# A routed expert layer on one core: the order of gathers, block products and weight loads around the second product

## The chip, the cores and the metric

The kernel runs on one core of a Trainium2 chip. The metric is the device time of one execution in microseconds (us); shown are the median of three executions and, from one further execution, a profile taken by the hardware profiler. TensorE (PE in the profile; its weight loads are PEld), VectorE (DVE), ScalarE (ACT) and GpSimd (POOL) each work through their own instructions in order and wait for one another by semaphores; SyncE (SP) only issues transfers.

## The reference

Linear attention without softmax gives 4608 rows of 512 numbers, and each row then goes through one of eight two-layer networks ("experts"), which a gate chooses:

```python
kv = einsum('bhsd,bhse->bhde', k, v)
out = einsum('bhsd,bhde->bhse', q, kv)
x = out / sqrt(mean(out * out, -1) + 1e-6) * g_norm      # rearranged to (4608, 512)
e_idx = argmax(x @ w_gate, 1)
gate_w = softmax probability of that expert
eom = sigmoid(x @ w_output_gate)
for e in range(8):
    mask = e_idx == e
    h = maximum(x[mask] @ w1[e], 0)        # 512 -> 1024
    out[mask] = gate_w * eom[mask, e] * (h @ w2[e])   # 1024 -> 512
```

All is fp32.

## The kernel before, in words

The first third (`p1_main`) computes the attention and the gate, and writes each row, with its norm factors and its scale, to a table in HBM. What the change touches comes after it, in the loop over `RUNS` at line 1225. A run is the work of one expert on its rows, in the order of how many rows the experts have: runs 0 and 1 share the first expert, runs 2 to 8 take the other seven, with 672, 632, 608, 592, 576, 576 and 544 rows. A run has three kinds of work.

**Rows.** `gather` (line 239) fetches the rows of a run by indirect DMA that GpSimd issues, one per tile of 128 rows, into the buffers `xg`. `scale_rows` (262, by `scale_heads`, 257) multiplies them on GpSimd by their norm factors, one instruction a tile. `settle` (250) is a drain on GpSimd behind the last gather; in this loop it is called for the rows of run 8, in run 7. `x_stage` (410) transposes two tiles on TensorE and splits them and the block sums into a rounded high part (ScalarE) and the remainder (VectorE); `x_sums` (472) splits the sums. Both run in the second product of the run before.

**First product.** fp32 is made from two rounded parts: high x high, high x low, low x high. The first product, `x @ w1`, is done by a scheme of seven block products in place of eight (`seven`, 488) over four chunks c of the hidden columns. It is a generator; each step issues one block product of six matmuls (`product`, 480) with what ScalarE and VectorE make of it. For a chunk the order is 11, S3, 12, S2, then `late3` and `late4` of the chunk before, then S1; chunk 0 has five steps, the others seven, and two steps, `late3(3)` and `late4(3)`, close the generator. `late3` adds to the accumulator `a`, of which ScalarE must have copied S1's value (`sn`, 550); `late4` adds to `d`, which VectorE must have read (551). The sums of W1's blocks are made on GpSimd (`w_sums`, 366, four instructions a chunk), and `w_split` (377) splits W1 and the sums.

**Second product.** `mm2` (562) goes over the row tiles of a run; for each of eight hidden blocks f it issues three matmuls into one of two PSUM buffers `y0`, `y1`, and behind them whatever was put down as the events of f. Then y is scaled to SBUF and scattered to the output by an indirect DMA on GpSimd. A last tile of at most 64 rows (`half`; runs 1, 2, 6, 7 and 8) has two halves in PSUM that are added, with a buffer `y2`.

The order is written out by hand. `begin(i, n)` issues n steps of run i's products; `put(tile, f, ...)` puts work into the events. In run i the first loop (1251) issues chunks 1 to 3 of the first product, with the split of W2's chunk (`split`, 203), the load of the next W1 (`wload`, 195, issued by SP), in chunk 2 the gathers of run i + 1, and in chunk 3 the sums of the next W1's chunk 0 and the scaling. `listing` (1143) is a generator of small VectorE steps for a list of overflowing experts. Chunk 0 of the next run's product is issued in the events of the last tile.

The buffers of W1, W2, their splits, `xg`, `sn`, `ct`, `y2` and others are 29 slots of one size. `take` (173) hands out the one that has been free longest in the order of the code, and the new user's instruction waits until the old user's last reader is through. So the order of the code also settles what a load or a gather waits for.

Of the kernel before, what the change touches and what calls it, by code (L numbers as in the profile page):

```python
# [135 lines left out]
def body(ctx: ExitStack, tc: tile.TileContext, kvm, rem, qT, wg, gn, w1, w2, kc, xs, tab, out):  # L136
# [425 lines left out]
    def mm2(i, k, events):  # L562
# [37 lines left out]
        if M == T:  # L600
            y2_ = take([P, 1024], F32, "y2")
            y2 = y2_[:, 0:DM]
            o = T if i > 1 else P // 2
            nc.scalar.copy(y2[:M], ps[o:o + M])
            nc.vector.tensor_tensor(out=y[:M], in0=ps[:M], in1=y2[:M], op=ALU.add)
            nc.vector.tensor_scalar(out=y[:M], in0=y[:M], scalar1=tl[:M, 0:1], scalar2=None, op0=ALU.mult)
            give(y2_)
        else:
            nc.scalar.activation(y[:M], ps[:M], AF.Copy, scale=tl[:M, 0:1])  # L609
# [4 lines left out]
        tc.add_to_no_dep_group("out", i_.ins)  # L614
        return i_
# [596 lines left out]
    with tc.manual_schedule(engines=MAN):  # L1212
# [12 lines left out]
        for i in range(len(RUNS)):  # L1225
# [23 lines left out]
            else:  # L1249

                for c in range(4):
                    if c:
                        begin(i, 2)
                        split(p, 2, c)
                        begin(i, 4)
                        if change:
                            wload(p + 1, 1, c - 1)
                        begin(i, 1)
                    else:
                        split(p, 2, c)  # L1260
                    if c == 2 and not last_run:
                        g_ = gather(i + 1)
                        if i + 2 == len(RUNS):
                            settle(g_)
                    if c == 3 and not last_run:
                        sums_of(p + 1, 0)
                        scale_rows(i + 1)
                    next(listing, None)
                    next(listing, None)
# [7 lines left out]
            if last_run and half(i):  # L1277
                order.insert(1, order.pop())
            if i > 1:
                put(order[0], 1, begin, i, 1)  # L1280
                put(order[0], 3, begin, i, 1)
                if change:
                    put(order[0], 3, wload, p + 1, 1, 3)
            if change:
                for c in range(4):
                    if c:
                        put(order[c - 1], 0, sums_of, p + 1, c)
# [4 lines left out]
                put(order[T - 1], 0, wload, p + 1, 2, 0)  # L1292
                for f, n in ((1, 1), (3, 2), (5, 1), (7, 1)):
                    put(order[T - 1], f, begin, i + 1, n)
# [9 lines left out]
            if i > 0:  # L1304
                for c in range(4):
                    drop(2, c)
            if change:
                for c in range(1, 4):
                    wload(p + 1, 2, c)
# [105 lines left out]
```

## Time and profile before

| | us |
|---|---|
| median of three executions | 585.17 (584.56 to 586.82) |
| the profiled execution | 586.47 |
| its span, first to last instruction | 584.7 |
| mean granted clock of TensorE | 0.975 of full speed |
| TensorE busy | 545.3 |
| VectorE busy | 378.5 |
| ScalarE busy | 299.4 |
| GpSimd busy | 258.4 |

Run 2's products begin in the last tile of run 1, near 178 us; the second product of run 7, with 8's first steps in it, ends near 535 us. How to read it: a row of the timeline has its start from the span's start, its duration, the engine, the line of the kernel and the operation; what stands in brackets is how long the engine stood idle before it and which instruction's end released it. A row of waits sums these idle times by waiting and releasing line. The granted clock is the share of its full speed of 2.4 GHz that TensorE was given in a stretch; 0.50 is its lower level of 1.2 GHz. A duration of matmuls is modelled at its end, so starts are the better guide.

### The profile page before, as it was taken

The numbers are of one execution on the slowest core, as the hardware profiler recorded it, in microseconds if no ns is written. First come the engines' busy times: TensorE is split into PE (matmuls) and PEld (weight loads), VectorE is DVE, ScalarE is ACT, GpSimd is POOL, SyncE is SP. The second block draws the span as 40 slices with busy tenths as digits, with TensorE's granted clock in tenths as the row PEclk, the third lists the DMA queues.
The fourth block names the chain that finished last, engine by engine and source line by source line (L and its number), as shares of the span: only waits on it lengthen the run. The fifth ranks groups of instructions, "written<-read, shape, count | busy, mean of one in ns | idle before, by whom it ended". The sixth has DMA issues, their size and how long they took to land.

```text
span 584.7 us, 10991 instructions
## 1 busy us (share of the span) xinstructions
PE 545.3 (93%) x4052; PEld 464.2 (79%) x4052; DVE 378.5 (65%) x897; ACT 299.4 (51%) x632; POOL 258.4 (44%) x280
## 2 busy tenths in 40 slices
PE   8899989999899969989999999989998999699995
PEld 6688877748788948879789878978896788588974
DVE  2135998855697798267955793669278947494610
ACT  1468764332575537245645482657365645374510
POOL 2001323178472466237743772487148722781011
PEclk9999997998999989999999999999999999799999
DMA  8999999945004600254054305511551236023001
GB/s 263 372 417 415 416 395 336 343 154 189 1 38 158 219 24 36 91 184 159 19 189 135 121 36 180 189 53 57 195 167 38 90 132 220 0 89 129 2 20 46
DMA packets 28744, 92.35 MB, mean 158 GB/s; under 512 B 4082, under 2 KB 4210, under 8 KB 28688
## 3 DMA queue, kind: packets, MB, share of 16 engines
q1 hardware_dynamic: 21952, 71.63, 33.6%
q0 software_dynamic: 6304, 19.78, 9.7%
q8 instruction: 33, 0.54, 0.4%
q10 hardware_dynamic: 432, 0.21, 0.1%
q14 instruction: 23, 0.19, 0.1%
HBM read 72.41 MB, written 19.78 MB: 158 GB/s over the span
## 4 chain that ended last, share of the span: by engine, by line
PE 56%; DVE 17%; DMA 11%; ACT 7%; issue 4%; POOL 2%; POOLq 1%; SPq 0%; DVEq 0%; ACTq 0%
PE yps L596 26%; PE hpsa L484 11%; PE hpsd L484 4%; DVE hT L507 4%; DMA ld<-kvm 3%; PE hps L484 3%; PE yps L590 3%; ACT hT L504 2%; PE yps L574 2%; PE tps L430 2%; DMA xs<-xrow 2%; DMA ld<-rem 2%; DVE wlo L229 2%; DMA wraw<-w 2%; PE ops L792 2%
## 5 line engine op out<-in xcount | busy, mean ns | idle before, releaser
L596 PE MATMUL yps<-whi,hT 128*128 128x512 f32 (+3 forms) x560 | 188.7, 401 | 7.9 <-ACT hT L504 4.8
L596 PEld LDWEIGHTS yps<-whi,hT 128*128 128x128 f32 (+3 forms) x560 | 104.7, 188 | 35.6 <-ACT hT L504 7.4
L610 POOL DMA_INDIRECT out<-y,oidx x42 | 57.3, 1365 | 164.7 <-ACT y L609 119.5
L596 PE MATMUL yps<-wlo,hT 128*128 128x512 f32 (+3 forms) x280 | 110.9, 396 | 0.0
L244 POOL DMA_INDIRECT xg<-xs,gidx x42 | 46.3, 1103 | 55.6 <-DMA xs<-xrow 14.4
L507 DVE SCALAR_TENSOR_TENSOR hT<-ct,hT 128x256 fp32r<-128x256 f32 (+6 forms) x88 | 46.3, 557 | 22.8 <-ACT hT L504 22.8
L596 PEld LDWEIGHTS yps<-wlo,hT 128*128 128x128 f32 (+3 forms) x280 | 52.6, 188 | 9.9
L504 ACT ACTIVATE hT<-ct 128x288 fp32r<-128x288 f32 (+11 forms) x56 | 34.6, 618 | 43.0 <-DVE ct L518 43.0
L229 DVE TENSOR_TENSOR wlo<-wraw,whi 128x1024 fp32r<-128x1024 f32 x32 | 43.5, 1359 | 12.3 <-ACT whi L226 12.2
L609 ACT ACTIVATE y<-yps,tl 128x512 f32<-128x512 f32 (+3 forms) x37 | 25.3, 685 | 49.3 <-PE yps L596 19.8
L484 PE MATMUL hpsa<-xT,wh 128*128 128x288 f32 (+5 forms) x224 | 48.1, 302 | 1.5 <-ACT sn L542 1.1
L484 PE MATMUL hpsd<-xT,wh 128*128 128x288 f32 (+5 forms) x224 | 48.0, 301 | 0.3 <-DVE xT L477 0.3
L484 PE MATMUL hpsa<-xb,wh 128*128 128x288 f32 (+5 forms) x224 | 47.6, 300 | 0.6 <-DVE hT L507 0.6
L818 DVE TENSOR_REDUCE ss<-sq 128x8 f32<-128x512 f32 x36 | 23.9, 681 | 33.2 <-ACT sq L808 33.2
L260 POOL TENSOR_TENSOR xg<-xg 128x512 f32<-128x512 f32 (+6 forms) x40 | 43.6, 1122 | 0.0
L792 PE MATMUL ops<-aug,ld 64*128 64x80 f32 (+1 forms) x640 | 41.5, 283 | 0.0
L388 DVE SCALAR_TENSOR_TENSOR wl<-wraw,gcol,wh 128x512 fp32r<-128x512 f32 (+1 forms) x56 | 40.7, 766 | 0.0
L484 PEld LDWEIGHTS hpsa<-xT,wh 128*128 128x128 f32 x224 | 37.1, 188 | 4.0 <-ACT sn L542 1.3
L484 PEld LDWEIGHTS hpsa<-xb,wh 128*128 128x128 f32 x224 | 37.2, 188 | 2.2 <-DVE hT L507 0.9
L792 PEld LDWEIGHTS ops<-aug,ld 64*128 64x128 f32 (+1 forms) x640 | 36.3, 188 | 3.1 <-issue 1.2
L484 PEld LDWEIGHTS hpsd<-xT,wh 128*128 128x128 f32 x224 | 37.2, 188 | 2.0 <-DVE xT L477 0.6
L388 DVE SCALAR_TENSOR_TENSOR wl<-ws,gcol,wh 128x1024 fp32r<-128x1024 f32 x28 | 38.1, 1360 | 0.1
(222 smaller groups left out, 1142.1 us busy)
## 6 DMA issues: line engine op xcount, KB each, us to landing
wraw<-w SPq DMA_DIRECT2D x64, 512.0 KB, 3.8
ld<-kvm SPq DMA_DIRECT2D x32, 512.0 KB, 9.9
ld<-qT SPq DMA_DIRECT2D x18, 512.0 KB, 10.5
xs<-xrow SPq DMA_DIRECT2D x9, 528.0 KB, 6.6
xs<-xrow SPq DMA_DIRECT2D x2, 1320.0 KB, 6.5
xs<-xrow SPq DMA_DIRECT2D x1, 2112.0 KB, 12.7
ld<-rem SPq DMA_DIRECT2D x3, 512.0 KB, 9.9
xg<-xs,gidx POOLq DMA_INDIRECT x42, 4.2
```

Source lines behind the costliest of these rows:

```text
L229: eng.tensor_tensor(out=lo, in0=r, in1=hi.bitcast(F32), op=ALU.subtract)
L244: gathered = nc.gpsimd.indirect_dma_start(out=x[:M, :], out_offset=None, in_=rows, in_offset=bass.IndirectOffsetOnAxis(ap=gidx[:M, p, t:t ...
L260: eng.tensor_tensor(out=v, in0=v, in1=f, op=ALU.mult)
L388: nc.vector.scalar_tensor_tensor(out=lo, in0=x, scalar=gcol[:, 0:1], in1=hi.bitcast(F32), op0=ALU.mult, op1=ALU.subtract)
L484: nc.tensor.matmul(ps, W[a][d], X[b][d], start=start and k == 0, stop=k == 5, skip_group_check=not start)
L504: S.activation(hh, x, AF.Relu)
L507: V.scalar_tensor_tensor(out=v(o, j1 - j0), in0=x[..., j0:j1], scalar=0.0, in1=hh[..., j0:j1].bitcast(F32), op0=ALU.max, op1=ALU.subtract)
L596: nc.tensor.matmul(ps[:M], a, b, start=(f == 0 and j == 0), stop=(f == 7 and j == 2))
L609: nc.scalar.activation(y[:M], ps[:M], AF.Copy, scale=tl[:M, 0:1])
L610: i_ = nc.gpsimd.indirect_dma_start(out=out, out_offset=bass.IndirectOffsetOnAxis(ap=oidx[:M, p, t:t + 1], axis=0), in_=y[:M], in_offset=N ...
L792: nc.tensor.matmul(v[r0:r0 + m, u, p, :], qt[g // 2][r, p, q0:q0 + m], augs[b % 3][r, p, :], start=True, stop=True)
L818: nc.vector.tensor_reduce(out=o, in_=sq, axis=AX.X, op=ALU.add)
```

## The change

The gathers of run i + 1 are issued after the split of chunk 2 and ahead of four more block products; the scaling follows in the same chunk and no longer behind the sums of W1's chunk 0. `late3(3)` and `late4(3)` come at events 0 and 1 of the first tile instead of 1 and 3, and the sums of W1's later chunks at event 1 instead of 0. The loads of W1's chunks come a chunk later, the last two together at event 1. In the last tile, W2's chunks are dropped at events 1, 3 and 5, each followed by the load of a chunk of the next W2; before, three of the loads came after the tile. The last step of chunk 0 of the next run (S1) comes in new events "8", behind y and its scatter. The half tile's y is scaled in the two instructions that add it, and the third is gone. The list's steps are one for each of chunks 1 to 3, where they were two for each of chunks 0 to 3.

```diff
@@ -601,9 +601,9 @@
             y2_ = take([P, 1024], F32, "y2")
             y2 = y2_[:, 0:DM]
             o = T if i > 1 else P // 2
-            nc.scalar.copy(y2[:M], ps[o:o + M])
-            nc.vector.tensor_tensor(out=y[:M], in0=ps[:M], in1=y2[:M], op=ALU.add)
-            nc.vector.tensor_scalar(out=y[:M], in0=y[:M], scalar1=tl[:M, 0:1], scalar2=None, op0=ALU.mult)
+            nc.scalar.activation(y2[:M], ps[o:o + M], AF.Copy, scale=tl[:M, 0:1])
+            nc.vector.scalar_tensor_tensor(out=y[:M], in0=ps[:M], scalar=tl[:M, 0:1], in1=y2[:M],
+                                           op0=ALU.mult, op1=ALU.add)
             give(y2_)
         else:
             nc.scalar.activation(y[:M], ps[:M], AF.Copy, scale=tl[:M, 0:1])
@@ -612,6 +612,8 @@
             in_=y[:M], in_offset=None, bounds_check=NTOK - 1, oob_is_err=False)
         tc.declare_no_dep(i_.ins, group="out", reason=nodep)
         tc.add_to_no_dep_group("out", i_.ins)
+        for e in events.get(8, ()):
+            e()
         return i_
 
 
@@ -1252,21 +1254,22 @@
                     if c:
                         begin(i, 2)
                         split(p, 2, c)
+                        if c == 2 and not last_run:
+                            g_ = gather(i + 1)
+                            if i + 2 == len(RUNS):
+                                settle(g_)
                         begin(i, 4)
-                        if change:
-                            wload(p + 1, 1, c - 1)
+                        if change and c > 1:
+                            wload(p + 1, 1, c - 2)
                         begin(i, 1)
                     else:
                         split(p, 2, c)
                     if c == 2 and not last_run:
-                        g_ = gather(i + 1)
-                        if i + 2 == len(RUNS):
-                            settle(g_)
-                    if c == 3 and not last_run:
+                        scale_rows(i + 1)
+                    if c == 3 and change:
                         sums_of(p + 1, 0)
-                        scale_rows(i + 1)
-                    next(listing, None)
-                    next(listing, None)
+                    if c:
+                        next(listing, None)
 
             at = {}
 
@@ -1276,22 +1279,27 @@
             order = list(range(T))
             if last_run and half(i):
                 order.insert(1, order.pop())
+            end = order[T - 1]
             if i > 1:
+                put(order[0], 0, begin, i, 1)
                 put(order[0], 1, begin, i, 1)
-                put(order[0], 3, begin, i, 1)
                 if change:
-                    put(order[0], 3, wload, p + 1, 1, 3)
+                    for c in (2, 3):
+                        put(order[0], 1, wload, p + 1, 1, c)
             if change:
                 for c in range(4):
                     if c:
-                        put(order[c - 1], 0, sums_of, p + 1, c)
+                        put(order[c - 1], 1, sums_of, p + 1, c)
                     put(order[c], 4 if c < T - 1 else 0, w_split, p + 1, c)
                 for k in range(3):
                     put(order[k], 2, x_stage, i + 1, k)
                     put(order[k], 7, x_sums, i + 1, k)
-                put(order[T - 1], 0, wload, p + 1, 2, 0)
-                for f, n in ((1, 1), (3, 2), (5, 1), (7, 1)):
-                    put(order[T - 1], f, begin, i + 1, n)
+                put(end, 0, wload, p + 1, 2, 0)
+                for c in range(3):
+                    put(end, 2 * c + 1, drop, 2, c)
+                    put(end, 2 * c + 1, wload, p + 1, 2, c + 1)
+                for f, n in ((1, 1), (3, 2), (5, 1), (8, 1)):
+                    put(end, f, begin, i + 1, n)
             for k in order:
                 g_ = mm2(i, k, at.get(k, {}))
                 if last_run and k == order[-3]:
@@ -1303,10 +1311,8 @@
                     stage(1, k)
             if i > 0:
                 for c in range(4):
-                    drop(2, c)
-            if change:
-                for c in range(1, 4):
-                    wload(p + 1, 2, c)
+                    if (2, c) in wgt:
+                        drop(2, c)
     main.close()
 
     with ExitStack() as p3:
```

## Rows read from the trace of the kernel before

**Rows 1.** The page: busy us (share of the span) and instructions of each engine.
```profile
PE 545.3 (93%) x4052; PEld 464.2 (79%) x4052; DVE 378.5 (65%) x897; ACT 299.4 (51%) x632; POOL 258.4 (44%) x280
```

**Rows 2.** Waits of PE, 180 to 560 us: us in total, times, longest us.
```profile
PE tps L430 <- POOL xg L260: 8.8, 8, 6.0
PE yps L596 <- ACT hT L504: 4.8, 4, 3.8
PE yps L596 <- DVE hT L507: 2.8, 4, 1.3
PE hps L484 <- DVE y L605: 2.5, 4, 0.7
PE hpsa L484 <- ACT sn L542: 1.1, 1, 1.1
PE hpsa L484 <- DVE hT L507: 0.6, 1, 0.6
PE hpsa L484 <- ACT sn L532: 0.3, 2, 0.2
```

**Rows 3.** Stretches: PE, PEld, DVE, ACT, POOL busy us, granted clock, DMA share, GB/s.
```profile
217.50:221.50 4.00, 3.89 (x9) 2.95 (x10) 3.78 (x6) 3.62 (x6) 0.10 (x1) 0.50 0.00 0
...
502.00:505.20 3.20, 3.20 (x13) 2.67 (x14) 1.31 (x6) 1.42 (x6) 3.20 (x4) 0.56 0.00 0
...
257.00:260.00 3.00, 1.91 (x12) 1.40 (x10) 1.97 (x4) 1.74 (x3) 2.59 (x2) 1.00 0.98 255
```

**Rows 4.** The chain that ended last, run 7: start us, us, what.
```profile
487.59 3.99 DMA xg<-xs,gidx
...
491.60 6.20 POOLq L252
...
500.87 1.01 POOL xg L260
...
505.13 0.80 PE hpsd L484 x6
```

**Rows 5.** Timeline of run 7: start us, us, engine line op [idle before].
```profile
481.38 1.00 POOL L244 DMA_INDIRECT xg<-xs,gidx  x1 [1.37 <-DVE hT L507]
...
482.49 0.83 DVE L507 SCALAR_TENSOR_TENSOR hT<-ct,hT 128x512 fp32r<-128x512 f32 x2 [0.79 <-ACT hT L504]
```

**Rows 6.** Timeline of PE, run 2's tiles 0 and 1.
```profile
213.27 0.50 PE L596 MATMUL yps<-whi,hT 128*128 128x512 f32 x1 [1.25 <-DVE hT L507]
...
217.61 0.79 PE L596 MATMUL yps<-whi,hT 128*128 128x512 f32 x1 [3.84 <-ACT hT L504]
```

**Rows 7.** Timeline of DVE, run 2.
```profile
198.40 0.93 DVE L507 SCALAR_TENSOR_TENSOR hT<-ct,hT 128x640 fp32r<-128x640 f32 x2 [0.88 <-ACT hT L504]
...
204.59 2.30 DVE L507 SCALAR_TENSOR_TENSOR hT<-ct,hT 128x640 fp32r<-128x640 f32 x2 [0.88 <-ACT hT L504]
...
209.04 0.15 DVE L1186 SCALAR_TENSOR_TENSOR c<-cf,fle 128x8 f32<-128x8 f32 x1
...
211.88 0.93 DVE L1195 TENSOR_TENSOR sel<-sel 128x352 f32<-128x352 f32 x1
```

**Rows 8.** Timeline of run 5, end of the products and tile 0.
```profile
380.86 1.23 DVE L229 TENSOR_TENSOR wlo<-wraw,whi 128x1024 fp32r<-128x1024 f32 x1 [0.73 <-ACT whi L226]
...
383.66 0.39 PE L596 MATMUL yps<-whi,hT 128*128 128x512 f32 x1
...
384.20 0.38 ACT L550 COPY sn<-hpsa 128x296 f32<-128x296 f32 x1
...
385.05 0.43 PE L484 MATMUL hpsa<-xb,wh 128*128 128x296 f32 x2
```

**Rows 9.** The chain that ended last, start of run 3.
```profile
254.07 3.32 DMA wraw<-w
```

**Rows 10.** Timeline of DVE, run 3.
```profile
268.57 0.48 DVE L507 SCALAR_TENSOR_TENSOR hT<-ct,hT 128x316 fp32r<-128x316 f32 x1
...
275.01 0.93 DVE L507 SCALAR_TENSOR_TENSOR hT<-ct,hT 128x316 fp32r<-128x316 f32 x1
```

## The prediction

> **What bounds the kernel now.** I read the shares of the engines first: TensorE is busy 93% of the span [rows 1], so a gain can only come from what stops it, not from less work on the others. Second, the list of its waits over the stretch of the seven block-product runs (180 to 560 us) [rows 2]: `xg` 8.8, the two rows of `yps` waiting for `hT` 4.8 + 2.8, the other four 4.5, 20.9 us in all. Third, the granted clock behind the two long waits [rows 3]: after the long one in run 2 TensorE works 4.0 us at 0.50, after the one in run 7 3.2 us at 0.56; where a wait was 1.1 us the clock stayed at 1.00. At the lower level (1.2 GHz instead of 2.4) these two stretches lose 4.0 x 0.50 = 2.0 us and 3.2 x 0.44 = 1.4 us. So some 24 us of the span are open to a reordering. I call the runs 2 to 8 as the code does; run 8 is the last.
>
> **Part 1: rows gathered and scaled sooner.** `x_stage` at event 2 of the first tile transposes rows that GpSimd must have scaled; that is the `tps <- xg` wait, 8.8 us in 8 places, of which run 7 alone has 6.0 [rows 2]. In run 7's chain the last gather takes 3.99 us, the drain of `settle` 6.20 us to 497.80, the four `ws` sums come next, and the first scaling only at 500.87 [rows 4]: 3.07 us of sums stand between the data and the work that TensorE waits for. The change puts the scaling ahead of these sums, and outside run 7 ahead of their wait for a slot too (they take the buffer of the last raw chunk of W2). The seven small waits, 8.8 - 6.0 = **2.8 us**, go.
>
> In run 7 less is won than the words promise. Following the list of free buffers through the code, all five gathers now take buffers of block chunk 0 (`ct`, `wh0`, `wl0`, `wh1`), and the first gets `ct`, which VectorE still reads in the instruction that ends at 482.49 + 0.83 = 483.32, while the first gather of before began at 481.38 [rows 5]. At 1.3 us a gather the fifth starts near 488.7, 1.1 us later than the 487.59 of before. Landing 3.99 and drain 6.20 are the same, so the first two row tiles are scaled (1.01 us each) at 499.95 and 501.0. TensorE stopped at 501.92 - 6.02 = 495.9; it now does the product `late4`, 0.80 us [rows 4], before that, and stops at 496.7. It waits 3.3 us and some 0.6 for the second tile, 3.9 in place of 6.0; I take **2.0 us** for run 7 and leave its 1.4 us of clock where it is. Bounds: nothing, if the drain grows with what it finds open; 6.0 + 1.4 = 7.4 if the drain is shorter.
>
> The sums of chunk 0 end later than before by at most the five scalings less the lead won; the reader is `w_split` at event 4. It lies behind `x_stage` on ScalarE and VectorE, which covers it outside run 7. The loads of W1 are issued one chunk later and the last two at event 1. SP has hardly anything else in its queue there, each load waits only for its buffer, and the sums that read them stand behind five scalings on GpSimd: cost nothing. If that cover is gone, GpSimd waits for a load, then `w_split`, then ScalarE's copy of y.
>
> **Part 2: `late3` and `late4` at events 0 and 1.** They were at 1 and 3, around `x_stage`, so ScalarE and VectorE did `x_stage` before they made the last two blocks of `hT`; TensorE then ran into these blocks at f = 6 and 7. In run 2 that was 1.25 us and 3.84 us [rows 6]; the two rows have 4.8 + 2.8 = 7.6 us in all [rows 2]. In run 2 there was more: the overflow list's five VectorE operations from 209.04 to 212.81 stood in the queue before `late3`'s block, beside slowed ones [rows 7]. With one step of the list for each chunk after the first, the heavy steps come in run 4, beside products. With the blocks made before `x_stage`, TensorE has the transposes and the matmuls of four values of f between `late4` and the first of these blocks, which covers them. I count **7.6 us**, and the 2.0 us of clock behind run 2's wait. Bounds: 2.5 if run 2's waits and its clock stay (9.6 - 5.1 - 2.0), 9.6 if all goes.
>
> A new wait comes with it. `late3` adds to the accumulator that ScalarE must first have copied. In run 5 the last product of the loop ended where tile 0 began, 383.66; six matmuls later, at 385.05, `late3` started; the copy ran from 384.20 to 384.58 [rows 8]. With three matmuls (0.69 us) between them TensorE would be there at 384.35 and wait 0.23 and a hand-over of about 0.1: 0.3 us in each of seven runs, **2.1 us lost**. Bounds: nothing where ScalarE is early; 0.7 each (4.9) if it is as late again.
>
> **Part 3: the last tile.** The y of the last tile is now written before the next run's `S1` work, and the half tile's y is ready after two steps, without the third. That was the wait `hps <- DVE y`, 2.5 us in four places, and `hpsa <- ACT sn L532`, 0.3 us [rows 2]: **2.8 us**. The next W2 is loaded from events 0, 1, 3 and 5 instead of after the tile, into buffers that are free by then. In run 2 chunk 1 of W2 had to wait for `y2`, and its load of 3.32 us from 254.07 [rows 9] is behind the waits `ACT sn L542` 1.1 and `DVE hT` 0.6 of [rows 2]: **1.7 us**. The drops are only of chunks whose last matmul has been issued. `S1` itself moves behind the scatter in the issue order alone; TensorE has it next as before. Bounds of this part: 0 to 4.5.
>
> **Contention, a cost the trace shows only elsewhere.** The scalings now run beside the last chunk of products instead of beside tile 0. In run 2 a pair of `hT` operations took 2.30 us where the same pair before it took 0.93 [rows 7]: +0.69 each, with GpSimd scaling. In run 3 one took 0.93 where its twin took 0.48 [rows 10]: +0.45. In the last chunk three VectorE operations read two SBUF tensors: two `hT`, then `wlo`. VectorE had 0.73 us idle before `wlo` [rows 8], so with 0.45 each the queue is late by 2 x 0.45 - 0.73 + 0.45 = 0.6 us; I take 0.7 for runs 3 to 6, because run 3 is nearest in shape, and 1.7 for run 2, whose `hT` are in pairs (5 x 0.69 = 3.4, less the same idle and the list's steps that leave). Run 7 scales after its drain, run 8 not at all. The delay passes through ScalarE's copies to `late3`: **4.5 us lost**. Bounds: 0, and rival (a).
>
> The Trainium skill ("SBUF — State Buffer", section "SBUF: two separate sides") says that VectorE with two SBUF inputs and GpSimd hold the shared port pair for a whole instruction, and the other blocks fully. By that rule each of those operations could stand behind a whole scaling, and the sum would be a gain of some 2 us instead of 12; the rows show less than that for the single operations, as the rule would if only a part of a scaling is left.
>
> **The sum.** 2.8 + 2.0 + 7.6 + 2.0 + 2.8 + 1.7 = 18.9 us won, 2.1 + 4.5 = 6.6 lost: 12.3 us. The profiled execution took 586.47 us (span 584.7 and 1.8 around it), so it would be 574.2; it lay 1.3 us above the median of the runs shown, 585.17, so the forecast is **572.9 us**.
>
> **The rivals.** (a) *Each operation waits for a whole scaling* of 1.01 us [rows 4]: 3 x 1.01 - 0.73 = 2.3 us in four runs, 5.1 in run 2, 14.3 us: gain 18.9 - 2.1 - 14.3 = 2.5, **582.7 us**, no change that can be told. For it: the pair in run 2. Against: +0.45 in run 3. (b) *Slower: `late3` stops the clock.* If three whole scalings (3 x 1.01) reach `late3` with nothing to absorb them, the wait at event 0 is near that of run 2 [rows 6] and its clock falls too, 3.0 + 2.0 us in each of the five runs that scale beside the last chunk: 25.0 us against 18.9 - 2.1 = 16.8, **593.4 us**. It decides from 16.8 / 5 = 3.4 us a run, clock included. For it: nothing stands between the last product and `late3` but three matmuls. Against: three delays of a whole scaling each would have to meet in every run. (c) *All of it goes*, run 7's wait and clock too (7.4 instead of 2.0), and no contention: 18.9 + 5.4 - 2.1 = 22.2, **563.0 us**. (d) *The change doesn't do what it says in run 7*: the gathers come later and nothing is won there. It is in my sum as 2.0; without it 574.9, inside the forecast's own case.
>
> **Chances.** Forecast with (d) 0.64, own range 567 to 579; (a) 0.12; (b) 0.09; (c) 0.15. Faster by over 0.5% (2.9 us, about what a measurement of this kernel tells from no change) is the forecast's case and (c) with a little of (a): 0.81; the rest of (a) is 0.10; (b) is 0.09. The range goes from (c) to just past (a): 562 to 583.5; (b) and the edges are left out.
>
> **What would show it.** Right: no `tps <- xg` wait but run 7's of 3 to 4 us; no wait on `hT` in tile 0 or 1 and a clock of 1.00 from 211 to 225 us; no `hps <- DVE y`; new waits of `hpsa` for `ACT sn L550` of 0.3 to 1.7 us at event 0. Wrong: `hpsa <- ACT sn` of over 3 us a run with the clock at 0.5 behind it, or a wait of `tps` for VectorE in tile 1 or 2, where the block sums would have become the bound, or run 7's drain beginning before 491.6 less the run's own lead.

## The result, and the profile after

The changed kernel takes 579.13 us (median of four executions, 576.71 to 579.88) against 585.91 us of the kernel before in the same comparison: 0.9879 of its time, 95% interval 0.9841 to 0.9917. It is faster by 6.8 us where 12.3 were forecast; the time lies inside the whole range, 6.2 us above the forecast and just above the 567 to 579 us that the forecast's own case was given. The profiled execution took 579.68 us, with a span of 577.8 us and a mean granted clock of 0.974 (before: 586.47, 584.7 and 0.975), so the two traces can be compared one to one.

From the page of the changed kernel: busy us, share and instructions of each engine, and the granted clock over 40 slices.

```profile
PE 541.4 (94%) x4052; PEld 466.4 (81%) x4052; DVE 388.3 (67%) x892; ACT 299.1 (52%) x632; POOL 253.8 (44%) x280
...
PEclk9999997999999999999999899989999999799999
```

TensorE has the same 4052 instructions as in [rows 1]. VectorE has five fewer and is busy 9.8 us longer (388.3 against 378.5): some of its work got slower.

The waits of TensorE in the changed kernel, 180 to 560 us (us in total, times, longest), to be laid beside [rows 2]:

```profile
PE hpsa L484 <- ACT sn L532: 6.2, 2, 3.2
PE tps L430 <- POOL xg L260: 5.8, 1, 5.8
PE hpsa L484 <- ACT sn L550: 2.1, 4, 1.1
PE hpsd L484 <- DVE ct L551: 1.5, 2, 0.9
PE tps L430 <- DVE xt L450: 0.6, 1, 0.6
```

Nearly all that stood in [rows 2] is gone: both rows of `yps` for `hT`, `hps` for `y`, `hpsa` for `sn` of line 542, and seven of the eight small waits for `xg`. The eighth, run 7's, is nearly as long as before (5.8 against 6.0). New at the top stands `hpsa <- ACT sn L532`, which had been 0.3 us: two waits of about 3 us. In sum 16.2 us instead of 20.9.

Stretches of the changed kernel (start:end, length, then busy us and instructions of PE, PEld, DVE, ACT and POOL, granted clock, DMA share, GB/s), answering to [rows 3]:

```profile
211.00:225.00 14.00, 13.37 (x65) 10.79 (x64) 13.75 (x38) 10.91 (x28) 6.72 (x8) 1.00 0.05 19
317.00:321.00 4.00, 3.96 (x15) 3.96 (x16) 3.23 (x6) 1.80 (x3) 1.38 (x3) 0.50 0.01 3
321.00:325.00 4.00, 4.00 (x21) 3.67 (x21) 2.59 (x5) 1.65 (x4) 3.92 (x6) 0.77 0.35 114
376.00:379.00 3.00, 2.94 (x16) 2.94 (x17) 2.96 (x4) 1.82 (x4) 2.67 (x3) 0.75 0.08 33
496.00:499.50 3.50, 3.28 (x12) 2.71 (x13) 1.35 (x6) 1.84 (x7) 3.50 (x5) 0.50 0.00 0
```

The first row is the stretch of run 2's long wait of before: now the clock is 1.00. The next three lie behind the two new waits, in runs 4 and 5, and lose 4.0 x 0.50 + 4.0 x 0.23 + 3.0 x 0.25 = 3.7 us. The last is run 7, 3.5 x 0.50 = 1.75 us.

Where the new waits come from is seen in the timeline of the changed kernel at the end of run 4's products (start, us, engine, line, operation, idle before and releaser):

```profile
311.79 5.60 POOL L260 TENSOR_TENSOR xg<-xg 128x512 f32<-128x512 f32 x5
...
312.07 4.42 DVE L507 SCALAR_TENSOR_TENSOR hT<-ct,hT 128x608 fp32r<-128x608 f32 x1 [0.83 <-ACT hT L504]
...
316.41 0.46 DVE L551 TENSOR_TENSOR ct<-hpsd,sn 128x304 f32<-128x304 f32 x1
316.58 0.41 ACT L532 COPY sn<-hpsa 128x304 f32<-128x304 f32 x1 [3.88 <-DVE hT L507]
...
317.05 0.87 PE L484 MATMUL hpsa<-xT,wh 128*128 128x304 f32 x2 [2.98 <-ACT sn L532]
```

Five scalings run on GpSimd without a gap, 5.60 us, and one VectorE operation beside them takes **4.42 us**. ScalarE's copy of block product 11 (`sn`, line 532) starts when that operation ends: in the code the `sn` of chunk 3 takes the slot that `ct` of chunk 1 gave back, and the operation on `hT` is the last reader of that `ct`. S2 adds to the accumulator that this copy reads, so TensorE waits 2.98 us, and its clock is then at 0.50. In run 5 it is the same operation again, beside four scalings:

```profile
370.84 4.04 POOL L260 TENSOR_TENSOR xg<-xg 128x512 f32<-128x512 f32 x4
...
370.92 4.60 DVE L507 SCALAR_TENSOR_TENSOR hT<-ct,hT 128x592 fp32r<-128x592 f32 x1 [0.80 <-ACT hT L504]
...
376.06 0.54 PE L484 MATMUL hpsa<-xT,wh 128*128 128x296 f32 x2 [3.25 <-ACT sn L532]
```

How long a run lasts shows what this is worth (my reading of the timelines, from the first matmul of a run's products to the first of the next run's):

| us | run 2 | 3 | 4 | 5 | 6 | 7 |
|---|---|---|---|---|---|---|
| before | 68.68 | 57.98 | 55.33 | 55.85 | 54.91 | 59.35 |
| changed | 62.54 | 53.31 | 59.25 | 58.02 | 54.18 | 58.81 |

Runs 2 and 3 won 6.14 + 4.67 = 10.8 us, near what the whole change was to win. Runs 4 and 5 gave 3.92 + 2.17 = 6.1 us back.

Last, the chain that ended last in the changed kernel, run 7 (start, us, what), beside [rows 4]:

```profile
482.61 6.19 DMA xg<-xs,gidx
...
488.83 6.20 POOLq L252
...
495.13 1.05 POOL xg L260
...
496.22 2.12 PE tps L430 x8
```

The scaling now follows the drain directly (495.13 behind 488.83 + 6.20), as intended, and the drain is the same 6.20 us. But the last gather's landing took 6.19 us where it took 3.99.

### The profile page after: what moved, and what is told of

Its sections match the earlier page's. It is cut to its first block, busy times and chain, and to the rows that moved or that the text cites. A ratio compares the mean times of both kernels' runs of the same rounds, so it can differ in the third digit from the quotient of the medians.

```text
span 577.8 us, 10976 instructions
## 1 busy us (share of the span) xinstructions
PE 541.4 (94%) x4052; PEld 466.4 (81%) x4052; DVE 388.3 (67%) x892; ACT 299.1 (52%) x632; POOL 253.8 (44%) x280
## 4 chain that ended last, share of the span: by engine, by line
PE 63%; DVE 15%; DMA 11%; ACT 4%; issue 3%; POOLq 1%; POOL 1%; SPq 0%; DVEq 0%; ACTq 0%
PE yps L596 29%; PE hpsa L484 13%; PE hpsd L484 6%; DVE hT L507 4%; DMA ld<-rem 4%; PE hps L484 3%; PE yps L590 3%; PE tps L430 3%; PE yps L574 2%; DMA xs<-xrow 2%; DVE wlo L229 2%; DMA xg<-xs,gidx 2%; ACT hT L504 2%; DMA ld<-kvm 2%; PE ops L794 2%
## 5 line engine op out<-in xcount | busy, mean ns | idle before, releaser
L596 PE MATMUL yps<-whi,hT 128*128 128x512 f32 (+3 forms) x560 | 185.7, 397 | 0.0
L610 POOL DMA_INDIRECT out<-y,oidx x42 | 52.3, 1246 | 156.1 <-ACT y L609 106.3
L244 POOL DMA_INDIRECT xg<-xs,gidx x42 | 44.4, 1056 | 67.6 <-DMA xs<-xrow 14.4
L507 DVE SCALAR_TENSOR_TENSOR hT<-ct,hT 128x256 fp32r<-128x256 f32 (+6 forms) x88 | 54.1, 644 | 22.9 <-ACT hT L504 22.9
L596 PEld LDWEIGHTS yps<-wlo,hT 128*128 128x128 f32 (+3 forms) x280 | 52.3, 187 | 10.1
L484 PE MATMUL hpsa<-xT,wh 128*128 128x288 f32 (+5 forms) x224 | 49.5, 309 | 6.2 <-ACT sn L532 6.2
L229 DVE TENSOR_TENSOR wlo<-wraw,whi 128x1024 fp32r<-128x1024 f32 x32 | 46.4, 1450 | 7.1 <-ACT whi L226 6.9
L484 PE MATMUL hpsa<-xb,wh 128*128 128x288 f32 (+5 forms) x224 | 49.0, 307 | 2.3 <-ACT sn L550 2.1
L484 PE MATMUL hpsd<-xT,wh 128*128 128x288 f32 (+5 forms) x224 | 49.3, 307 | 1.7 <-DVE ct L551 1.5
L484 PEld LDWEIGHTS hpsa<-xT,wh 128*128 128x128 f32 x224 | 38.6, 196 | 8.2 <-ACT sn L532 6.7
```

Source lines behind the costliest of these rows:

```text
L229: eng.tensor_tensor(out=lo, in0=r, in1=hi.bitcast(F32), op=ALU.subtract)
L244: gathered = nc.gpsimd.indirect_dma_start(out=x[:M, :], out_offset=None, in_=rows, in_offset=bass.IndirectOffsetOnAxis(ap=gidx[:M, p, t:t ...
L484: nc.tensor.matmul(ps, W[a][d], X[b][d], start=start and k == 0, stop=k == 5, skip_group_check=not start)
L507: V.scalar_tensor_tensor(out=v(o, j1 - j0), in0=x[..., j0:j1], scalar=0.0, in1=hh[..., j0:j1].bitcast(F32), op0=ALU.max, op1=ALU.subtract)
L596: nc.tensor.matmul(ps[:M], a, b, start=(f == 0 and j == 0), stop=(f == 7 and j == 2))
L610: i_ = nc.gpsimd.indirect_dma_start(out=out, out_offset=bass.IndirectOffsetOnAxis(ap=oidx[:M, p, t:t + 1], axis=0), in_=y[:M], in_offset=N ...
```

## The experiments

Two theories for the 6 us that were given back, and for why only runs 4 and 5 lose them. **H, the held operation:** VectorE's operation on two SBUF tensors stands through the scalings, and the reuse of `ct`'s slot carries this to S2; in runs 4 and 5 alone, because the overflow list holds a slot there, which shifts what every later `take` gets and lets the gathers, and with them the scalings, come earlier. **L, the list:** its VectorE steps, now one in each of chunks 1 to 3 until the eleventh in run 5, are in the way in runs 4 and 5, and had been the cause of run 2's wait before. A third question is run 7. All diffs are against the changed kernel.

**1. No scaling for the rows gathered in runs 4 and 5.**

```diff
-                    if c == 2 and not last_run:
+                    if c == 2 and not last_run and i not in (4, 5):
                         scale_rows(i + 1)
```

> This kernel is the changed one with the scaling left out of runs 4 and 5 (the rows of runs 5 and 6 stay unscaled). Theory H (held): the two long waits of the changed kernel, 2.98 and 3.25 us of S2 for ScalarE's copy (hpsa <- ACT sn L532), come from VectorE's hT operations of 4.42 and 4.60 us, which stand behind GpSimd's scalings that follow one another without a gap. Then both waits are under 0.3 us, the two hT operations are back at about 0.8 us, the clock stays at 1.00 behind them, and the span is 6 to 9 us shorter than the 577.8 of the changed kernel. Theory L (list): the heavier steps of the overflow list, which now fall into runs 4 and 5, fill VectorE's queue. Then both waits stay at 2 us or more and the span is within 2 us of 577.8.

One execution: 565.93 us (kernel before in the same comparison: 585.62). Its waits of TensorE, 180 to 560 us:

```profile
PE tps L430 <- POOL xg L260: 5.1, 1, 5.1
PE hpsa L484 <- ACT sn L550: 2.3, 5, 1.1
...
```

The row of line 532, which had stood first, is not in the list at all. Without scalings beside it the operation takes 0.80 us in run 4 and is not held. The time is 13.2 us under that of the changed kernel, but not all of it is the scalings': run 2's products begin at 173.56 us and not at 175.47, ahead of anything that the edit touches. Runs 4 and 5 themselves are 5.5 and 4.7 us shorter, 53.74 and 53.29 us. So their scalings cost some 10 us, of which 6.2 stand in the list of waits. The list's steps were all still there.

**2. The list's steps all in the last run.**

```diff
-                    if c:
-                        next(listing, None)
+                    if last_run:
+                        for _ in range(3):
+                            next(listing, None)
```

> All steps of the overflow list are issued in run 8, three for each chunk. Theory L: the waits hpsa <- ACT sn L532 (6.2 us in all) are gone and the time is 6 to 8 us under the changed kernel's 579.1, near 572. Theory H: the list itself costs nothing, but its buffer no longer shifts the order of free buffers in runs 4 and 5, so the gathers there begin later, as in run 6, and with them the scaling; the holds of VectorE fall elsewhere. Waits of 1 to 2 us a run as in run 6 (1.05 + 0.86) in place of 3, so 575 to 579, with some hT or wlo operation of over 2 us still in each of runs 2, 4, 5 and 6.

571.85 us, ratio 0.9768 [0.9728, 0.9807]: 7.3 us less than the changed kernel, which is the time that L forecast, while H's was missed. The waits on line 532 are gone; in run 8, where all the steps now stand together, TensorE got waits of 1.05, 0.60 and 2.43 us. But the edit takes away two things at once: the steps, and the slot that the list holds from run to run. It does not tell H from L; experiment 6 does.

**3. The sums of W1's chunk 0 ahead of the scaling again.**

```diff
-                    if c == 2 and not last_run:
-                        scale_rows(i + 1)
                     if c == 3 and change:
                         sums_of(p + 1, 0)
+                    if c == 3 and not last_run:
+                        scale_rows(i + 1)
```

> The changed kernel with the sums of chunk 0 ahead of the scaling again, as before the change; all else stays. Theory H: the scaling starts after wlo of chunk 3 and falls beside x_stage, so no hT operation in the last chunk is over 2.5 us and the waits for ACT sn L532 (6.2), ACT sn L550 (2.1) and DVE ct L551 (1.5) fall to under 3 us in all; back come waits of x_stage for the scaling, 0 to 0.6 us a run in runs 2 to 6, and run 7's wait is about 3 us longer (8 to 9). Time 573 to 577. Theory L: the waits for ACT sn L532 stay at 5 us or more and the time is 580 or more.

573.08 us, 0.9782 [0.9752, 0.9811], as H forecast: undoing this half of part 1 wins 6.1 us. Its waits of TensorE:

```profile
PE tps L430 <- POOL xg L260: 9.0, 4, 8.1
PE hpsd L484 <- DVE ct L551: 1.3, 2, 0.9
PE hpsa L484 <- ACT sn L550: 1.3, 4, 0.7
...
```

No wait on line 532: the sums come first, and the scalings no longer meet the critical operation. Run 7 loses 8.1 - 5.8 = 2.3 us, since its scaling again stands behind the sums, and of the small waits only three come back, 9.0 - 8.1 = 0.9 us in all.

**4. Run 7's drain behind the sums.**

```diff
                             g_ = gather(i + 1)
-                            if i + 2 == len(RUNS):
-                                settle(g_)
...
                     if c == 3 and change:
                         sums_of(p + 1, 0)
+                    if c == 3 and i + 2 == len(RUNS):
+                        settle(g_)
```

> The changed kernel with the drain of run 7 moved behind the scaling and the sums of chunk 0. If the 6.20 us of the drain are what run 7's transposes wait for, their wait falls from 5.77 us to under 1 us, the clock behind it stays at 1.00, and the time is 6 to 8 us under the changed kernel, 571 to 573. A new wait of up to 2 us may come in tile 1 or 2 of run 7, where the sums of chunk 1 now stand behind the drain and w_split behind them. If the wait is one for the landing of the gathers instead (6.19 us after the last was issued), it stays at 4 us or more.

572.19 us, 0.9763 [0.9722, 0.9803], 6.9 us under the changed kernel. Its waits of TensorE:

```profile
PE hpsa L484 <- ACT sn L532: 6.3, 2, 3.3
PE hpsa L484 <- ACT sn L550: 3.2, 5, 1.1
PE hps L484 <- ACT y L609: 1.6, 1, 1.6
...
```

The wait for `xg` is gone altogether: the drain guards only the rows of run 8, and when it stands behind the scalings nothing waits for it but sums and scatters. It costs 1.6 us elsewhere. The two waits on line 532, those of runs 4 and 5, are unchanged, as they should be. So the drain's place was worth about 7 us net: the stop's 5.8 us and the 1.75 us of clock behind it, less the new wait, account for 6.0 of them.

**5. The list's steps away from runs 4 and 5**, six in runs 2 and 3 and the other five in the third tile of run 8:

```diff
-                    if c:
+                    if c and i < 4:
                         next(listing, None)
...
+            if last_run:
+                for _ in range(5):
+                    put(order[2], 0, next, listing, None)
```

> Steps 1 to 6 of the list stay in runs 2 and 3, steps 7 to 11 (with the list's buffer) move into the second product of run 8, where VectorE is idle. Both theories: no wait for ACT sn L532 in runs 4 and 5, and without the waits that the list made in run 8 in the run before (1.05 + 0.60 + 2.43 us) the time is 3 to 6 us under that run's 571.9: 566 to 569.

568.58 us, 0.9717 [0.9692, 0.9742], as forecast, 10.6 us under the changed kernel. No wait on line 532 and none in run 8. As in experiment 2, steps and slot go together.

**6. The slot without the list:** list as in experiment 2, but a buffer is taken in run 4 and given back in run 5, with one small memset as its only work.

```diff
+                    if i == 4 and c == 1:
+                        kept = take([P, 1024], F32, "kept")
+                        nc.vector.memset(kept[:, 0:8], 0.0)
+                    if i == 5 and c == 2:
+                        give(kept)
```

> All list steps in run 8 as in the run before, but a buffer is taken in run 4 and given back in run 5 at the places where the list took and gave its own (one small memset uses it). So the order of free buffers in runs 4 and 5 is that of the changed kernel, with no list step there. Theory H: the gathers begin early again, the scalings come without a gap just ahead of an hT operation, which takes over 4 us in run 4 and in run 5, and the waits hpsa <- ACT sn L532 are back with 2.5 to 3.5 us each. Theory L: no such wait, as when the list was in run 8.

One execution: 584.27 us. The timeline of run 4 in this kernel:

```profile
310.78 5.04 POOL L260 TENSOR_TENSOR xg<-xg 128x512 f32<-128x512 f32 x5
...
311.27 5.21 DVE L507 SCALAR_TENSOR_TENSOR hT<-ct,hT 128x608 fp32r<-128x608 f32 x1 [0.83 <-ACT hT L504]
...
316.56 0.41 ACT L532 COPY sn<-hpsa 128x304 f32<-128x304 f32 x1 [4.66 <-DVE hT L507]
...
317.03 0.87 PE L484 MATMUL hpsa<-xT,wh 128*128 128x304 f32 x2 [3.76 <-ACT sn L532]
```

Not one step of the list is in runs 4 and 5, and the whole stop is back, longer than before: 5.21 us on VectorE, 3.76 us on TensorE, and 12.4 us more than experiment 2. Together with experiment 1 this settles it for H: what counts in runs 4 and 5 is which slots the gathers and `sn` get. Why the operation is held for so long there is another question, which it does not answer.

**7. `late3` and `late4` at events 1 and 3 again.**

```diff
-                put(order[0], 0, begin, i, 1)
                 put(order[0], 1, begin, i, 1)
+                put(order[0], 3, begin, i, 1)
```

> The changed kernel with late3(3) and late4(3) back at events 1 and 3. By the prediction's part 2: the waits for late3 and late4 (ACT sn L550 2.1, DVE ct L551 1.5) shrink to under 1.5 us, the waits of yps for the last blocks of hT come back with 0.5 to 1 us in four or five runs, without run 2's 5.1 us if it was the list that made these. So 579 to 582. If the order of these two alone had made run 2's wait, it is back with its clock, and the time is 584 to 587.

587.86 us, 1.0029 [1.0004, 1.0053]: 8.7 us lost. That is not the 579 to 582 us expected first but the second case, 584 to 587, and a little over it. Its waits of TensorE:

```profile
PE yps L596 <- ACT hT L504: 9.2, 5, 3.4
...
PE yps L596 <- DVE hT L507: 0.7, 2, 0.4
PE hpsa L484 <- ACT sn L550: 0.3, 1, 0.3
```

The waits of [rows 2] on `hT` are back, 9.9 us, and the price of the new order, `sn L550`, falls from 2.1 to 0.3. Run 2's long wait is among them (3.41 us at 213.26, against 3.84 in [rows 6]), although only light steps of the list stand in run 2 here, and the clock behind it is at 0.50 again. So the order of `late3` and `late4` makes the long wait without the heavy steps. The 1.25 us ahead of it in [rows 6] do not come back; a share of the list, which the prediction had named, is left open for those alone.

**8. The last tile as before:** three instructions for the half tile's y, `S1` at event 7, W2's chunks dropped and loaded after the tile.

```diff
-            nc.scalar.activation(y2[:M], ps[o:o + M], AF.Copy, scale=tl[:M, 0:1])
-            nc.vector.scalar_tensor_tensor(out=y[:M], in0=ps[:M], scalar=tl[:M, 0:1], in1=y2[:M],
-                                           op0=ALU.mult, op1=ALU.add)
+            nc.scalar.copy(y2[:M], ps[o:o + M])
+            nc.vector.tensor_tensor(out=y[:M], in0=ps[:M], in1=y2[:M], op=ALU.add)
+            nc.vector.tensor_scalar(out=y[:M], in0=y[:M], scalar1=tl[:M, 0:1], scalar2=None, op0=ALU.mult)
...
-                for c in range(3):
-                    put(end, 2 * c + 1, drop, 2, c)
-                    put(end, 2 * c + 1, wload, p + 1, 2, c + 1)
-                for f, n in ((1, 1), (3, 2), (5, 1), (8, 1)):
+                for f, n in ((1, 1), (3, 2), (5, 1), (7, 1)):
...
+            if change:
+                for c in range(1, 4):
+                    wload(p + 1, 2, c)
```

> The changed kernel with the last tile as before: y behind S1's work, the three steps of the half tile's y, three of W2's loads after the tile. By the prediction's part 3: waits hps <- DVE y of 0.5 to 0.8 us in four places come back (2.5), 0.3 for ACT sn, and 1.7 at the start of run 3 if a W2 chunk takes y2's buffer again. Time 581 to 584.

583.19 us, 0.9955 [0.9938, 0.9971]: part 3 is worth 583.19 - 579.13 = 4.1 us. Of its waits, the one that the part was to remove is back to the tenth of [rows 2]:

```profile
PE hps L484 <- DVE y L605: 2.5, 4, 0.7
```

The 1.7 us at the start of run 3 did not come back (neither `sn L542` nor `hT` is in the list), so what there is beyond the 2.5 us isn't the load of W2's chunk 1 as the prediction had it.

**9. Experiments 4 and 5 in one**, with the drain in the fourth tile of run 7:

```diff
-                            if i + 2 == len(RUNS):
-                                settle(g_)
...
-                    if c:
+                    if c and i < 4:
                         next(listing, None)
...
+            if i + 2 == len(RUNS):
+                put(order[3], 0, settle, g_)
+            if last_run:
+                for _ in range(5):
+                    put(order[2], 0, next, listing, None)
```

> The kernel with the list late, and run 7's drain moved to event 0 of its fourth tile, behind all sums. The wait of run 7's transposes (4.8 us there) and the clock behind it go, without the wait for y that came when the drain stood behind the first sums (1.6 us): 568.6 - 4.8 - 1.5 = 562, so 561 to 564. If the drain only moves its cost, a wait of 4 us or more appears in run 7's last tiles and the time is 566 or more.

562.14 us, 0.9587 [0.9557, 0.9617], as forecast. It is 17.0 us under the changed kernel, where the parts alone had 10.6 + 6.9 = 17.5: the two losses are independent.

**10. The same, and the sums ahead of the scaling** (the diff of experiment 3 on top).

> As the run before, and the sums of chunk 0 ahead of the scaling. Theory H: the waits for ACT sn L550 and DVE ct L551 (3.0 + 1.3 us with the list late) fall to about 2.5, the waits of x_stage for the scaling are about 1 us in all, so the time is within 2 us of the run before, 560 to 564. It is 565 or more if the sums first make run 7's transposes wait as they did with the drain ahead of them.

**560.12 us, 0.9546 [0.9509, 0.9582]**, the fastest of all, 19.0 us under the changed kernel and 25.7 under the one before. All its waits of TensorE from 180 to 560 us:

```profile
PE hpsa L484 <- ACT sn L550: 0.7, 4, 0.2
PE hpsd L484 <- DVE ct L551: 0.5, 2, 0.2
PE yps L596 <- DVE hT L507: 0.4, 1, 0.4
PE tps L430 <- DVE xt L450: 0.3, 1, 0.3
```

1.9 us in place of 16.2. And the timeline of its run 5, where scalings still meet VectorE:

```profile
370.55 0.89 DVE L507 SCALAR_TENSOR_TENSOR hT<-ct,hT 128x592 fp32r<-128x592 f32 x1 [0.81 <-ACT hT L504]
...
370.77 6.34 POOL L260 TENSOR_TENSOR xg<-xg 128x512 f32<-128x512 f32 x5
...
374.79 1.42 DVE L507 SCALAR_TENSOR_TENSOR hT<-ct,hT 128x592 fp32r<-128x592 f32 x1 [0.84 <-ACT hT L504]
```

Five scalings again, but the operations of the same shape, those of the two later chunks, take 0.89 and 1.42 us and not 4.60, and the scalings take 6.34 us for five instead of 4.04 for four: here the two engines alternate.

**11. The gathers behind S1 again**, the scaling right after them.

```diff
-                        if c == 2 and not last_run:
-                            g_ = gather(i + 1)
-                            if i + 2 == len(RUNS):
-                                settle(g_)
...
                     if c == 2 and not last_run:
+                        g_ = gather(i + 1)
+                        if i + 2 == len(RUNS):
+                            settle(g_)
                         scale_rows(i + 1)
```

> The changed kernel with the gathers back behind S1 of chunk 2, the scaling directly behind them. If the buffers and not the place in the code set when gathers begin, the fifth begins within 1.5 us of where it did, and run 7's wait stays at 4.5 to 6.5 us. By theory H the two long waits in runs 4 and 5 depend on how the scaling meets the hT operation: with other buffers and the last gather later, they change by over 1 us each or vanish. Time 572 to 580. If the earlier place was the gain, waits of x_stage for the scaling come back in runs 2 to 6 with 0.3 us or more each, and the time is over 580.

583.82 us, 0.9957 [0.9925, 0.999], a miss of the 572 to 580 us forecast. Its waits of TensorE:

```profile
PE hpsa L484 <- ACT sn L550: 6.7, 6, 3.2
PE hpsa L484 <- ACT sn L532: 5.5, 2, 2.7
PE tps L430 <- POOL xg L260: 2.6, 2, 2.2
...
```

The operation on `hT` is still held, 4.20 and 4.09 us, where I had expected it to change by over 1 us: a gather that comes later in the code doesn't part it from the scalings. And `late3` now waits up to 3.2 us, in run 2, with the clock at 0.50 behind it, which is rival (b)'s mechanism in one run. Run 7 is the one part that behaved: its first gather no longer takes `ct`'s slot, the last gather lands in 4.97 us, and TensorE waits 2.2 us.

**12. A 0.1 us memset on GpSimd behind each scaling**, to see whether a gap lets VectorE in.

```diff
             scale_heads(xg[(RUNS[i][0], t)][:M], nc.gpsimd)
+            if i > 2:
+                gap = cst.tile([P, 1], F32, name="gap", bufs=1)
+                nc.gpsimd.memset(gap, 0.0)
```

> The changed kernel with a memset of one column on GpSimd behind each scaling from run 3's on (rows of run 3 and later). If VectorE's operation is held because the scalings follow one another without a gap, and an instruction that reads no SBUF tensor is a gap, the hT operations of 4.42 and 4.60 us fall to under 2.2 us (one scaling) and the two waits of 2.98 and 3.25 to under 1.2. If GpSimd keeps its hold from instruction to instruction whatever it does, both operations stay over 4 us.

One execution: 582.59 us. The timeline of its run 4 (three added lines move L507 to L510):

```profile
315.77 1.06 POOL L260 TENSOR_TENSOR xg<-xg 128x512 f32<-128x512 f32 x1
...
316.04 4.52 DVE L510 SCALAR_TENSOR_TENSOR hT<-ct,hT 128x608 fp32r<-128x608 f32 x1 [0.83 <-ACT hT L507]
...
316.75 0.11 POOL L269 MEMSET gap<- 128x1 f32 x1
...
320.25 1.21 POOL L260 TENSOR_TENSOR xg<-xg 80x512 f32<-80x512 f32 x1 [0.31 <-DMA xg<-xs,gidx]
```

The first case did not come: the operation still stands through four scalings and four memsets, and ends at 320.56, just behind the 0.31 us in which GpSimd itself waits for the last gather. A memset between two scalings is no gap.

## Why the prediction was right in its direction, and the gain put nearly twice too high

**Right: parts 2 and 3, and the small waits.** The waits on `hT` are gone, and the clock from 211 to 225 us is 1.00. `late3`'s new wait for `sn` measured 2.1 us, which is the 2.1 of the sum, but by luck: instead of 0.3 us in each of seven runs there are four waits, 0.71 and 1.05 us in runs 2 and 6 beside scalings and under 0.2 in runs 7 and 8; in experiment 10 the same four come to 0.7 us. So the price of the order itself is about a third of what was forecast, and the rest stands beside scalings. Net of that price part 2 was put at 7.6 + 2.0 - 2.1 = 7.5 us; undoing it cost 8.7. Part 3 was put at 4.5 us; undoing it cost 4.1, though not by its own reckoning: 2.5 us are where it said, the 1.7 at the start of run 3 are not. The seven small waits are gone as forecast. With the gathers late and the scaling first (experiment 11) none returns outside run 7, and with the gathers early and the sums first (experiment 3) only 0.9 us do: the order of scaling and sums is enough by itself, and the earlier gathers do most of it too.

**Wrong: the contention, in size and place.** The step that failed is "I take 0.7 for runs 3 to 6 [...] The delay passes through ScalarE's copies to `late3`: 4.5 us lost". Each operation was given +0.45 us from [rows 10]. Measured, one operation in each of runs 4 and 5 took 4.42 and 4.60 us, against 0.8 us without scalings beside it. It did not reach TensorE at `late3` but a few products earlier, at S2, and by a path that the prediction didn't follow: it had traced the list of free slots for the gathers of run 7, and not for `sn`. The two stops cost 6.2 us of waiting and 3.7 us of clock, 9.9 us in place of 1.4. Set against run lengths this agrees: from experiment 10, where nothing is held, to the changed kernel, runs 4 and 5 differ by 59.25 - 53.79 + 58.02 - 53.37 = 10.1 us.

Rival (a) had the right mechanism at too low a price, and rival (b), `late3` stopping the clock, the right kind of stop at the wrong place. Two of the prediction's own signs of being wrong showed it: a wait of over 3 us for ScalarE's `sn` with the clock low behind it (line 532, and not `late3`'s 550), and a wait of `tps` for VectorE, 0.6 us in run 2. The Trainium skill ("SBUF — State Buffer", section "SBUF: two separate sides") says that of a VectorE operation with two SBUF inputs and a GpSimd operation, the one that starts first holds the shared ports for its whole instruction. The alternation in experiment 10 agrees with that, 1.42 us being one operation and part of one scaling. The 4.4 to 5.2 us in runs 4 and 5 do not: there the operation stood through three to five instructions of GpSimd.

**Wrong: run 7.** Forecast a wait of 3.9 us, measured 5.8. Run 7 starts 5.79 us earlier than before (462.76 against 468.55); with that added, the fifth gather began at 482.61 + 5.79 = 488.4 (forecast 488.7), TensorE stopped at 490.45 + 5.79 = 496.2 (forecast 496.7), and the drain took 6.20. The one step that failed is "Landing 3.99 and drain 6.20 are the same": the landing took 6.19, 2.2 us more, which is the missing 1.9. The mean DMA share is 0.96 between 482.6 and 488.8, where it was 0.62 in the landing of 3.99 us before and 0.70 in that of 4.97 us in experiment 11 (stretches of the kernel before and of the changed one, columns as above):

```profile
487.60:491.60 4.00, 4.00 (x32) 4.00 (x32) 2.87 (x7) 2.94 (x7) 0.85 (x1) 1.00 0.62 214
...
482.60:488.80 6.20, 6.01 (x42) 5.41 (x41) 4.57 (x13) 3.22 (x7) 1.05 (x1) 1.00 0.96 341
```

The loads of W1, moved in the same change to come a chunk later, are issued just then, all four between 478.98 and 486.5. No run moved these loads alone, so that they slowed the landing is likely but not shown.

**The sum again.** By the waits and the clock, contention cost 9.9 us in runs 4 and 5 and 1.5 + 0.6 = 2.1 in the two small new rows (`ct`, `xt`), 12.0 instead of 4.5 (leaving `late3`'s 2.1 where the sum had it), and run 7 fell short by 1.9: 9.4 us in all. Yet only 12.3 - 6.8 = 5.5 us of gain are missing. Part 2 gave 1.2 more than its term and part 3 0.4 less; some 3 us more were won than any row names. They are found in no wait: TensorE's busy time, as the profile models it, fell by 3.9 us (545.3 to 541.4) with the same 4052 instructions, and in runs 3 and 6, with the clock at 1.00 before and after, by 54.40 - 53.16 = 1.2 and 53.17 - 52.27 = 0.9 us. No term of the prediction has this, so a part of the 6.8 us is luck.

**What stays open.** Why an operation is held through several scalings in runs 4 and 5 and through one at most in run 3 or in experiment 10. In all the held cases the scalings follow each other directly behind a gather's issue (0.03 us in runs 4 and 5). Run 3 of the changed kernel, which also has three scalings in a row and an operation of 0.82 us among them, is no exception to this:

```profile
261.54 1.41 POOL L260 TENSOR_TENSOR xg<-xg 128x512 f32<-128x512 f32 x1 [0.72 <-DMA xg<-xs,gidx]
263.10 3.93 POOL L260 TENSOR_TENSOR xg<-xg 128x512 f32<-128x512 f32 x3 [0.16 <-DMA xg<-xs,gidx]
```

There one scaling follows the last gather directly, GpSimd then waits twice, and the operation begins at 264.07, 4.34 us behind that gather's issue. The traces of all fourteen kernels agree, from 180 to 560 us: of the 224 operations on `hT` or `wlo` that meet scalings, 43 were passed by at least one scaling that began after them and ended before them, and each of these began between 0.54 us before and 0.92 us after the end of the last gather's issue; of the 177 that began later, none was passed. That is a regularity of these traces and not a cause: the same few places come back in every kernel, and no run moved the distance between the gathers and the scaling alone. It does agree with experiments 3 and 10, where the sums stand between the two. Experiments 11 and 12, which left the scaling directly behind the gathers, left the hold. Open too is why TensorE's busy time fell: the listed waits fell by 20.9 - 16.2 = 4.7 us and the span by 6.9, and the clock explains no gain, its mean being the same.

## What to carry to other kernels

Before work is moved to a second engine's idle time, look at which operations of the first it will stand beside, and price the contention as a whole streak of instructions and not by the mildest pair in the trace; here it was worst where the streak followed directly behind the issue of a gather on the same engine, and other work put between them (experiment 3) won 6.1 us. Where buffers come from one list, follow the list for every user behind the moved line: here `sn` inherited `ct`'s slot, and a slow VectorE operation two steps away became a TensorE stop. And a drain belongs behind all that doesn't need it: moving one instruction (experiment 4) won as much as the whole change.

## What the runs showed of the hardware

A VectorE operation of 0.8 us on two SBUF tensors took 4.42, 4.60 and 5.21 us beside scalings of about 1.0 us on GpSimd (changed kernel and experiment 6), and a 0.1 us memset between the scalings didn't free it (4.52 us). In all traces here such an operation was passed by a later scaling only if it began within 1 us of the end of the last gather's issue (43 of 224); those that began later took turns with the scalings, 1.42 us in experiment 10. Its neighbours that read from PSUM were not stretched: `ct` from `hpsd` took 0.46 us right behind it. A stop of TensorE of 2.98 us was followed by a granted clock of 0.50; one of 1.6 us (experiment 4) was followed by 1.00. The drain took 6.20 us before and after, behind landings of 3.99 and 6.19 us, and the landing itself went from 3.99 to 6.19 us as the DMA share rose from 0.62 to 0.96.
